# Attention and mixture of experts in one kernel: the last four attention pairs run without an expert phase between them

## The chip, the cores and the metric

The kernel runs on one NeuronCore of one Trainium2 chip. The metric is the time of one execution on the device in microseconds (us). A profile is one execution recorded by the hardware: every instruction with its engine, start and duration, and every DMA packet. The engines are named as in the profile: PE (TensorE matmul), PEld (its weight load), DVE (VectorE), ACT (ScalarE), POOL (GpSimd), SP (SyncE, which issues DMAs here). "L407" is line 407 of the kernel. Each engine executes its own instructions in the order in which they were issued to it.

## The reference, cut to what matters

Multi-query attention (16 heads, one key and value head for each of 8 batches, 384 positions, head size 64) gives 3072 tokens of 1024 features. Each token then passes a two-level gate: the best of 4 groups, and the best of 4 experts in it. The chosen expert is two 1024x1024 matrices with a ReLU between them.

```python
scores = scale * np.matmul(q, k.transpose(0, 1, 3, 2))
attn = softmax(scores)
x = np.matmul(attn, v)            # as (3072, 1024)
g_idx = np.argmax(x @ w_group, axis=1)
for g in range(G):
    xg = x[g_idx == g]
    e_idx = np.argmax(xg @ w_expert[g], axis=1)
    for e in range(Eg):
        h = np.maximum(xg[e_idx == e] @ w1[g, e], 0.0)
        out[tokens] = (g_w * e_w)[:, None] * (h @ w2[g, e])
```

All tensors are fp32. The kernel computes attention and gates in fp32 and the experts in bf16.

## The kernel before

**Pairs.** The attention is cut into 24 pairs p = 3b + st, for batch b (0 to 7) and a third st (0 to 2) of its 384 queries. A pair has six steps j. `scores(p, j)` makes scores for 64 keys (four matmuls, shown by the profile as eight) and ACT takes their exponential into a `pt` tile. `values(p, j)` multiplies it with v. `pre_add` sums the six `pt` tiles on DVE, `fold_keys`, `join` and `invert` make the reciprocal row sums, and `weigh` writes the result to `xT`; POOL casts it to the bf16 tile `xbf` (L301), and after the third of a batch SP stores that to the DRAM buffer `x_bf` (L303). The loop of pair p runs the scores of p together with the values of p - 1.

**Gates.** `gate_a` multiplies `xT` with the gate weights (64 matmuls in the profile, L312). `choose_a` takes the first third of a batch alone, `counts(now, ...)` counts its tokens by expert with a matmul (L338), and `choose_b` picks the most frequent expert, reads its number into a register of POOL and issues the load of its weights from POOL: w1 in four pieces of 512 KB (L145) and w2 in one piece of 2048 KB (L357), sizes as they arrive in SBUF, in bf16; in DRAM they are fp32 and twice as large. `gate_logits`, `gate_math` and `counts(..., full)` do the rest of a batch's gates once all three thirds exist. The weight pool has two buffers for w1 and two for w2.

**Expert units.** One batch has 14 units in a list that `fill(n)` takes from: eight h units (L407, one 128-row block of the hidden layer, eight matmuls) and six y units (L417, half of the 1024 outputs of 128 tokens, eight matmuls). They are y00, y01, y10, y11, y20, y21 by third and half below. SP stores a third after its second half (L441).

**Phases.** Six times, after pairs 4, 7, 10, 13, 16 and 19, one batch's 14 units run as a phase, and the gates of the next batch are placed inside it. After pair 22 there is a shorter phase of the eight h units of batch 6, with the gates of batch 7 inside. The order of the rest is written out by hand after the loop: the remaining units of batch 6 and the 14 of batch 7, mixed with the values of pair 23, the last gates, and the leftover pair.

**The leftover pair.** Tokens that did not choose their batch's main expert form (batch, expert) pairs. `early_pair` finds one such pair and reads its number into registers of POOL, DVE and SP. `leftover_w1` and `leftover_w2` load its expert's weights from POOL (L145, L574): the first is called once all h units of batch 6 have run (it takes that batch's w1 buffer), the second once batch 6 has finished (it takes its w2 buffer). The pair's batch is read back from `x_bf` as `xe` (L656), its tokens are turned (`pb`, L717), ranked and picked (`pr` L672, `pg` L691, `px` L726), and passed through the expert: `ph` (L735, reads w1), `phT` (L741), `py` (L749, reads w2). The result `yc` goes to the tokens in two ways: an indirect DMA of POOL to DRAM (L755) for all tokens but the last 128, and for those 128 `spread` (matmuls `lo`, L458), whose result is added when y20 and y21 of batch 7 are written (`merge`, L449). Any further pair is left to a conditional block at the end.

Of the kernel before, what the change touches and what calls it, by code (L numbers as in the profile page):

```python
# [13 lines left out]
P = 128  # L14
# [7 lines left out]
def kernel(  # L22
# [25 lines left out]
    CW = 512  # L48
# [27 lines left out]
    def side(shape, dtype, name):  # L76
        return ps_s.tile(shape, dtype, tag="s", name=name)
# [351 lines left out]
    def first_units(b):  # L429
        rows = {}  # L430

        def place(st, cs):
            if cs.start == 0:
                rows[st] = pool.tile([P, Dm], FP32, tag="y", bufs=3, name="y")
            return rows[st][:, cs]

        def store(st, cs, y):
            if closes(st):
                nc.sync.dma_start(out=outv[b, :, st, cs], in_=y)
            elif cs.stop == Dm:  # L440
                nc.sync.dma_start(out=outv[b, :, st, :], in_=rows[st][:])  # L441

        def closes(st):
            return b == B - 1 and st == ST - 1

        def merge(st, cs, ps, y):
            if not closes(st):
                return False
            nc.vector.scalar_tensor_tensor(out=y, in0=ps[:], scalar=gsel[b][:, st:st + 1], in1=leftover["y"][:, cs], op0=OP.mult, op1=OP.add)  # L449
            return True  # L450
        return moe_units(wts[b][0], wts[b][1], xbf[b], lambda: gsel[b], place, store, merge, lambda st, nh: 2 if closes(st) and nh == 1 else 1)

    def spread():
        lo = [ps_m.tile([P, 2, CW], FP32, tag="o", name="lo"), side([P, 2, CW], FP32, "lo2")]
        for i in range(2):
            for c in (i, 2 + i):
                r = slice(CAP * c, CAP * c + CAP)
                nc.tensor.matmul(out=lo[c // 2][:, c % 2, 0:QW], lhsT=leftover["spread"][r, :], rhs=leftover["yc"][r, :], start=True, stop=True, tile_position=(CAP * c, 0))  # L458
        t = pool.tile([P, Dm], FP32, tag="pt", bufs=9, name="yl")
        for i in range(2):  # L460
            nc.scalar.copy(out=t[:, i * CW:(i + 1) * CW].rearrange("p (c n) -> p c n", c=2), in_=lo[i][:, :, 0:QW])
        leftover["y"] = t
# [13 lines left out]
    def fill(n):  # L476
        while n > 0:
# [10 lines left out]
            if ran[0] == (FO + 2 * ST) * (B - 1):  # L488
                leftover_w2()

    def gates(b):
        if b == 0:
            choose_a(0, gate_a(0, 0, 1))
            return
        ps = gate_a(b, 0, ST)
        choose_a(b, ps)
        gate_logits(b - 1, ps, 1, ST)
        gate_math(b - 1)
# [25 lines left out]
    PHASES[ST + 1] -= 3  # L524
    PHASES[NP - 2] = FO

# [9 lines left out]
    def early_pair():  # L536
        last = B - 1
        mask = pool.tile([P, GE], FP32, tag="mask", bufs=1, name="mask1")
        idf = pool.tile([P, 1], FP32, tag="idf", bufs=1, name="idf1")
        nc.vector.tensor_copy(out=idf[:], in_=choice[last][:, 0:1])  # L540
        nc.vector.tensor_scalar(out=mask[:], in0=iota16[:], scalar1=idf[:, 0:1], scalar2=None, op0=OP.is_equal)
        nc.vector.scalar_tensor_tensor(out=extra[:, last * GE:NPAIR], in0=seen[last], scalar=0.0, in1=mask[:], op0=OP.is_gt, op1=OP.subtract)
        known = pool.tile([P, 1], FP32, tag="known", bufs=1, name="known")
# [32 lines left out]
    for p in range(NP):  # L576
        b, st = divmod(p, ST)
        jobs = [lambda: gates(0), lambda: None, lambda: counts(0, None)] if p == 2 else []
        if p == 0 or p == ST or (st == 1 and 1 < b < B - 1):
# [14 lines left out]
        for j in range(KB):  # L594
            if p > 0:
                values(p - 1, j)
            if j == 2 and p > 0:
                join(p - 1)
            if j + 3 < KB:
                scores(p, j + 3)  # L600
            if 0 < j < 4:
                pre_add(p, j + 2)
            if j == 2 and p > 0:
                invert(p - 1)
            if j == 3:
                stats_q(p)
                if p == 1:
                    turn_q(2, lambda h: q_raw[0][:, 2, h], [nc.scalar.copy])
                elif p == 2:
                    turn_q(3, lambda h: q_nat[0][:, h], [nc.scalar.copy])  # L610
            if jobs:
                jobs.pop(0)()
            if p == ST + 1 and j == 0:
                fill(3)
            if st == 1 and 0 < b < B - 1 and j == 0:
                load_k(b + 1)
            if 0 < j < 5:
                some_q(1 if p <= ST + 1 else 2)
            if st == 1 and b + 1 < B and j == KB - 1:
                load_v(b + 1)  # L620
        assert not jobs
        if p > 0:
            weigh(p - 1)
        fold_keys(p)
        if st == 2 and b + 1 < B:
            stats_k(b + 1)
        if p in PHASES:
            n = PHASES[p]
            steps = {}
            prep_q(p + 1)  # L630
            if b == B - 1:
                steps = {1: lambda: gates(b), 2: lambda: counts(b, None), 3: lambda: (counts(None, b - 1), early_pair())}
            else:
                steps = {2: lambda: gates(b), 4: lambda: (counts(b, b - 1), turns(p))}
            for i in range(n):
                fill(1)
                if i in steps:
                    steps[i]()
    fill(3)
    for j in range(KB):  # L640
# [4 lines left out]
    weigh(NP - 1)  # L645
    last = B - 1
    fill(2)
    gate_logits(last, gate_a(last, 1, ST), 1, ST)
    gate_math(last)
    bound_a()  # L650
    fill(2)
    counts(None, last)
    bound_b()

    xe = pool.tile([P, KO, S], BF16, tag="qraw", bufs=2, name="xe")
# [11 lines left out]
    nc.vector.tensor_add(out=mb[:, 1, 3:4], in0=mb[:, 1, 2:3], in1=m[:, 2:3])  # L667
    nfl = pool.tile([P, 1], FP32, tag="nfl", bufs=1, name="nfl")
    nc.vector.reduce_sum(out=nfl[:], in_=extra[:], axis=AX)
    fill(1)  # L670
# [4 lines left out]
    nc.vector.tensor_copy(out=rk[:], in_=pr[:, 0:4])  # L675

    small = pool.tile([P, 2], FP32, tag="small", bufs=1, name="small")
# [4 lines left out]
    for st in range(ST):  # L682
        nc.vector.tensor_scalar(out=pick[:, st, :], in0=rank_of[:], scalar1=rk[:, st:st + 1], scalar2=m[:, st:st + 1], op0=OP.is_equal, op1=OP.mult)
    pick_bf = pool.tile([P, ST, CAP], BF16, tag="kT", name="pick_bf")
    nc.vector.tensor_copy(out=pick_bf[:], in_=pick[:, :, 0:CAP])
    of_last = pool.tile([P, 2, P], FP32, tag="presum", bufs=1, name="of_last")
    nc.vector.tensor_scalar(out=of_last[:, 0, :], in0=pick[:, ST - 1, :], scalar1=leftover["final"][:, 0:1], scalar2=None, op0=OP.mult)
    fill(2)
    pg = side([P, CW], FP32, "pg")
    for st in range(ST):  # L690
        nc.tensor.matmul(out=pg[:, 0:2], lhsT=pick[:, st, :], rhs=gi[:, st, :], start=(st == 0), stop=(st == ST - 1))  # L691
    gc = pool.tile([P, 2], FP32, tag="gc", bufs=1, name="gc")
    nc.vector.tensor_copy(out=gc[:, 0:1], in_=pg[:, 0:1])
    nc.vector.tensor_scalar(out=gc[:, 1:2], in0=pg[:, 1:2], scalar1=4.0, scalar2=quarter[:, 0:1], op0=OP.mult, op1=OP.add)
    rows = pool.tile([P, 1], U32, tag="rows", bufs=1, name="rows")
    nc.vector.tensor_copy(out=rows[:], in_=gc[:, 1:2])

    nc.tensor.transpose(out=pg[:, P:2 * P], in_=of_last[:, 0, :], identity=ident[:])
    nc.vector.tensor_copy(out=of_last[:, 1, :], in_=pg[:, P:2 * P])
    leftover["spread"] = of_last[:, 1, :]  # L700

    nc.vector.tensor_sub(out=small[:, 1:2], in0=nfl[:], in1=small[:, 0:1])
    nex = pool.tile([1, 1], I32, tag="nex", bufs=1, name="nex")
# [6 lines left out]
    nc.vector.tensor_copy(out=rarei[:], in_=raref[:, 0:1])  # L710
    fill(1)

    xtok = []
    for st in range(ST):
        pb = side([P, Dm], BF16, "pb")
        for ko in range(KO):
# [3 lines left out]
        xtok.append(xt)  # L720
        fill(1)
    assert len(units) == 2 * ST
    px = side([P, KO, CAP], FP32, "px")
# [5 lines left out]

    fill(1)  # L730
    w1c, w2c = leftover["w1"], leftover["w2"]
# [11 lines left out]
    nc.vector.tensor_copy(out=hc[:], in_=phT[:])  # L743
    fill(1)
    py = side([P, QW], FP32, "py")
# [5 lines left out]
    nc.scalar.activation(out=yc[:], in_=py[:], func=ACTF.Copy, scale=gc[:, 0:1])  # L751
    leftover["yc"] = yc
    fill(1)
    spread()
    nc.gpsimd.indirect_dma_start(out=out4[0:4 * (N - P)], out_offset=bass.IndirectOffsetOnAxis(ap=rows[:], axis=0), in_=yc[:], in_offset=None, bounds_check=4 * (N - P) - 1, oob_is_err=False)  # L755
    fill(1)
    rare = nc.values_load(rarei[0:1, 0:1], min_val=0, max_val=2, skip_runtime_bounds_check_because="a sum of two comparisons")  # L757
    fill(1)

    def load_pair(pair):  # L760
# [145 lines left out]
```

## Time and profile before

| | |
|---|---|
| time, three runs | 463.19, 463.54, 464.66 us (median 463.54) |
| profiled execution | 463.94 us; span of the core 462.4 us |
| PE busy | 449.4 us, 97% |
| DVE busy | 308.8 us, 67% |
| ACT busy | 241.6 us, 52% |
| POOL busy | 60.4 us, 13% |
| DMA | 74.55 MB by the packets, mean 161 GB/s |

"Busy" is time in which at least one instruction ran; a line such as "L407 PE MATMUL hps<-xbf,w x512 | 87.3, 326" says that 512 matmuls of that line took 87.3 us in union and 326 ns in the mean each (they overlap). Times within the execution count from its first instruction. A DMA queue's share is the busy time of its packets over 16 engines; it can pass 100%, since packets overlap.

### The profile page before, as it was taken

How to read it: one execution, taken by the hardware profiler on the slowest of the kernel's cores; microseconds unless marked ns; L12 is line 12 of the kernel's file. 1: busy time of each engine (PE TensorE's matmuls, PEld its weight loads, DVE VectorE, ACT ScalarE, POOL GpSimd, SP SyncE). 2: the span in 40 equal slices, each digit the busy share in tenths (PEclk: the TensorE clock that was granted, in tenths of full speed). 3: DMA queues.
4: the chain of work that ended last, by engine and by line, in shares of the span. 5: the costliest groups of instructions: out<-in, count | busy, mean ns of one | idle time of the engine just before them, and what ended most of it. 6: DMA issues, size and time to landing. Idle time of an engine off the chain costs nothing. (4 is left out here: it accounts for less than half of the span.)

```text
span 462.4 us, 10190 instructions
## 1 busy us (share of the span) xinstructions
PE 449.4 (97%) x4196; PEld 200.4 (43%) x4208; DVE 308.8 (67%) x489; ACT 241.6 (52%) x345; POOL 60.4 (13%) x83
## 2 busy tenths in 40 slices
PE   8999999999999999999999999999999999999893
PEld 6334445333643345433543336433453335434551
DVE  4899965499708985199834997089852999554511
ACT  2966643676347743566436763477435664532231
POOL 1004003000210103000030002101030001501000
PEclk9999999999999999999999999999999999999998
DMA  8688997997599296993979566992969910999952
GB/s 164 92 141 116 217 215 106 262 191 150 95 197 251 53 205 93 246 197 89 152 121 272 109 139 106 216 243 44 199 100 252 188 69 2 162 217 268 270 134 104
DMA packets 152454, 74.55 MB, mean 161 GB/s; under 512 B 120256, under 2 KB 138944, under 8 KB 152400
## 3 DMA queue, kind: packets, MB, share of 16 engines
q0 software_dynamic: 28416, 37.81, 48.0%
q1 hardware_dynamic: 122656, 35.68, 33.0%
q8 instruction: 35, 0.57, 0.5%
q10 hardware_dynamic: 1328, 0.33, 0.4%
q14 instruction: 19, 0.16, 0.1%
HBM read 92.62 MB, written 19.01 MB: 241 GB/s over the span
## 5 line engine op out<-in xcount | busy, mean ns | idle before, releaser
L253 ACT ACTIVATE pt<-s 128x1024 f32<-128x1024 f32 x144 | 142.1, 1026 | 71.9 <-PE s L251 71.2
L251 PE MATMUL s<-qT,kT 64*64 64x512 f32 x1152 | 142.4, 594 | 0.3 <-ACT qT L229 0.2
L290 PE MATMUL o<-pt,v 64*64 64x512 f32 x1152 | 141.1, 590 | 0.0
L261 DVE TENSOR_TENSOR presum<-presum,pt 128x1024 f32<-128x1024 f32 x96 | 116.6, 1215 | 15.2 <-ACT pt L253 9.8
L407 PE MATMUL hps<-xbf,w 128*128 128x384 bf16 x512 | 87.3, 326 | 0.4 <-ACT hT L408 0.4
L417 PE MATMUL yps<-w,hT 128*128 128x512 bf16 (+1 forms) x380 | 84.6, 375 | 0.6
L259 DVE TENSOR_TENSOR presum<-pt 128x1024 f32<-128x1024 f32 x24 | 29.4, 1223 | 76.8 <-ACT pt L253 75.4
L290 PEld LDWEIGHTS o<-pt,v 64*64 64x64 f32 x1152 | 43.4, 133 | 76.8 <-issue 73.0
L251 PEld LDWEIGHTS s<-qT,kT 64*64 64x64 f32 x1152 | 40.8, 133 | 66.8 <-issue 60.0
L407 PEld LDWEIGHTS <-w 128*128 128x128 bf16 x512 | 48.1, 98 | 38.1 <-issue 7.3
L301 POOL CAST xbf<-xT 128x1024 bf16<-128x1024 f32 x24 | 25.0, 1041 | 302.7 <-DVE xT L300 302.7
L419 ACT ACTIVATE y<-yps,gsel 128x512 f32<-128x512 f32 x46 | 31.6, 687 | 56.9 <-PE yps L417 55.3
L408 ACT ACTIVATE hT<-hps 128x384 bf16<-128x384 f32 x64 | 31.2, 488 | 55.6 <-PE hps L407 52.4
L417 PEld LDWEIGHTS <-hT 128*128 128x128 bf16 x392 | 37.7, 98 | 44.6 <-issue 2.4
L145 POOL DMA_DIRECT2D w<-in_moe_w_dram x36 | 24.8, 707 | 58.1 <-DVE gsel L395 37.7
L300 DVE TENSOR_TENSOR xT<-o,rinv 128x1024 f32<-128x1024 f32 x24 | 29.2, 1215 | 2.5 <-PE o L290 2.5
L280 DVE STREAM_TRANSPOSE rinv<-rc 128x1024 f32<-128x1024 f32 x24 | 29.9, 1245 | 0.8
L265 DVE TRANSPOSE_TENSOR_REDUCE fold<-presum 128x32 f32<-128x1024 f32 x24 | 29.6, 1232 | 0.0
L243 DVE STREAM_TRANSPOSE qT<-qraw 128x1024 f32<-128x1024 f32 x20 | 23.6, 1202 | 0.0
L209 ACT ACTIVATE qraw<-qraw 128x1024 f32<-128x1024 f32 x21 | 22.0, 1049 | 0.0
L273 PEld LDWEIGHTS sm<-fold,sel 64*64 64x64 f32 x192 | 7.3, 133 | 13.3 <-issue 13.3
L312 PE MATMUL gps<-xT,gw 128*32 128x96 f32 (+2 forms) x576 | 12.6, 239 | 0.0
(152 smaller groups left out, 152.9 us busy)
## 6 DMA issues: line engine op xcount, KB each, us to landing
w<-in_moe_w_dram POOLq DMA_DIRECT2D x36, 512.0 KB, 11.3
w<-in_moe_w_dram POOLq DMA_DIRECT2D x9, 2048.0 KB, 25.9
out_dram<-y SPq DMA_DIRECT2D x23, 512.0 KB, 6.9
qraw<-in_q_dram SPq DMA_DIRECT2D x56, 192.0 KB, 3.6
x_bf<-xbf SPq DMA_DIRECT2D x8, 768.0 KB, 4.0
v<-in_v_dram SPq DMA_DIRECT2D x16, 96.0 KB, 3.1
k<-in_k_dram SPq DMA_DIRECT2D x28, 48.0 KB, 2.7
qn<-in_q_dram SPq DMA_DIRECT2D x4, 256.0 KB, 5.2
```

The lines of the kernel that those rows point to most:

```text
L251: nc.tensor.matmul(out=ps[64 * c:64 * c + 64, a, :], lhsT=kT[b][r, j * D:(j + 1) * D], rhs=qT[p][r, c * CW:(c + 1) * CW], start=True, stop ...
L253: nc.scalar.activation(out=t[:], in_=ps[:], func=ACTF.Exp, scale=scale)
L259: nc.vector.tensor_add(out=presum[p][:], in0=pt[p, 0][:], in1=pt[p, 1][:])
L261: nc.vector.tensor_add(out=presum[p][:], in0=presum[p][:], in1=pt[p, j][:])
L265: nc.vector.tensor_reduce(out=fold[p][:], in_=presum[p][:].rearrange("p a (n i) -> p (a n) i", i=32), axis=AX, op=OP.add, apply_transpose= ...
L280: nc.vector.transpose(out=t[:].rearrange("p (b i) -> p b i", i=32), in_=rc[:].rearrange("p c b -> p (c b)").unsqueeze(2).to_broadcast([P, ...
L290: nc.tensor.matmul(out=o_ps[p][64 * a:64 * a + 64, c, :], lhsT=v_sb[b][r, j, :], rhs=pt[p, j][r, a, :], start=(j == 0), stop=(j == KB - 1))
L300: nc.vector.tensor_mul(out=xT[b][:, :, ts], in0=o_ps[p][:].rearrange("p c (h n) -> p (c h) n", n=P), in1=rinv[p][:].rearrange("p (h n) -> ...
L407: nc.tensor.matmul(out=ps[:, 0:S], lhsT=w1[:, ko, fc * P:(fc + 1) * P], rhs=xb[:, ko, :], start=(ko == 0), stop=(ko == KO - 1))
L408: nc.scalar.activation(out=state["h"][:, fc, :], in_=ps[:, 0:S], func=ACTF.Relu)
L417: nc.tensor.matmul(out=ps[:], lhsT=state["h"][:, fo, st * P:(st + 1) * P], rhs=w2[:, fo, cs], start=(fo == 0), stop=(fo == FO - 1))
L419: nc.scalar.activation(out=y, in_=ps[:], func=ACTF.Copy, scale=gs_of()[:, st:st + 1])
```

## The change

The phase after pair 22 is taken out, so that pairs 20 to 23 follow each other, and the units of batches 6 and 7 (28) stand after the loop.

- The gates of batch 7 stand inside pair 23: `gate_a` at step 2 behind `scores(23, 5)`, `choose_a` at the same step, the logits of batch 6 at step 4, and `counts(7, None)`, with the weight load that it issues, behind step 5.
- `prep_q(23)`, a transpose on DVE, moves from the phase to the end of pair 20.
- `early_pair` moves from the phase to behind `counts(None, 7)`, eight units into the run, and loses the five DVE instructions that gave it batch 7's flags from the first third alone; the reduction `nfl` goes, `known` serves in its place.
- Ahead of `py` stand 26 of the 28 units, where before it was 25: y11 is moved ahead of `py`. `ph` stands behind 22 units (before: 23), `px` behind 15 (before: 22).
- The indirect DMA stands right behind `yc` instead of behind `spread`, and `spread` stands behind y20 instead of ahead of it.
- The merge with `lo` is split: y20 is scaled by ACT as other units, DVE adds `lo` to it and SP stores it (`spread`), and only y21 merges as before; ACT copies half of `lo`.

```diff
         def store(st, cs, y):
             if closes(st):
-                nc.sync.dma_start(out=outv[b, :, st, cs], in_=y)
+                if cs.start == 0:
+                    leftover["row"] = y
+                else:
+                    nc.sync.dma_start(out=outv[b, :, st, cs], in_=y)
...
         def merge(st, cs, ps, y):
-            if not closes(st):
+            if not closes(st) or cs.start == 0:
                 return False
...
-        t = pool.tile([P, Dm], FP32, tag="pt", bufs=9, name="yl")
-        for i in range(2):
-            nc.scalar.copy(out=t[:, i * CW:(i + 1) * CW].rearrange("p (c n) -> p c n", c=2), in_=lo[i][:, :, 0:QW])
+        row = leftover["row"]
+        nc.vector.tensor_add(out=row.rearrange("p (c n) -> p c n", c=2), in0=row.rearrange("p (c n) -> p c n", c=2), in1=lo[0][:, :, 0:QW])
+        nc.sync.dma_start(out=outv[B - 1, :, ST - 1, 0:CW], in_=row)
+        t = pool.tile([P, CW], FP32, tag="pt", bufs=9, name="yl")
+        nc.scalar.copy(out=t[:].rearrange("p (c n) -> p c n", c=2), in_=lo[1][:, :, 0:QW])
...
     PHASES[ST + 1] -= 3
-    PHASES[NP - 2] = FO
...
+            if p == NP - 1 and j == 2:
+                gps = gate_a(b, 0, ST)
...
+            if p == NP - 1 and j == 2:
+                choose_a(b, gps)
...
+            if p == NP - 1 and j == 4:
+                gate_logits(b - 1, gps, 1, ST)
         assert not jobs
+        if p == NP - 1:
+            counts(b, None)
...
+        if p == NP - 4:
+            prep_q(NP - 1)
...
-            if b == B - 1:
-                steps = {1: lambda: gates(b), 2: lambda: counts(b, None), 3: lambda: (counts(None, b - 1), early_pair())}
...
-    fill(3)
+    last = B - 1
+    fill(2)
+    gate_math(last - 1)
     for j in range(KB):
...
     weigh(NP - 1)
-    last = B - 1
-    fill(2)
-    gate_logits(last, gate_a(last, 1, ST), 1, ST)
-    gate_math(last)
     bound_a()
+    fill(1)
+    counts(None, last - 1)
+    fill(1)
+    rest_of_gates(last)
+    bound_b()
     fill(2)
     counts(None, last)
-    bound_b()
-
+    early_pair()
+    fill(2)
     xe = pool.tile([P, KO, S], BF16, tag="qraw", bufs=2, name="xe")
...
     for st in range(ST):
+        fill(1)
         pb = side([P, Dm], BF16, "pb")
...
-        fill(1)
-    assert len(units) == 2 * ST
+    fill(1)
     px = side([P, KO, CAP], FP32, "px")
...
-    fill(1)
+    fill(FO - 1)
     w1c, w2c = leftover["w1"], leftover["w2"]
     ph = side([P, QW], FP32, "ph")
...
-    fill(1)
+    fill(3)
     py = side([P, QW], FP32, "py")
...
     leftover["yc"] = yc
+    nc.gpsimd.indirect_dma_start(out=out4[0:4 * (N - P)], ...)
     fill(1)
     spread()
-    nc.gpsimd.indirect_dma_start(out=out4[0:4 * (N - P)], ...)
-    fill(1)
     rare = nc.values_load(rarei[0:1, 0:1], ...)
     fill(1)
```

More of the change, by code (lines that the diff above doesn't have):

```diff
@@ L435, in place, with closes @@
             return rows[st][:, cs]
+        def closes(st):
+            return b == B - 1 and st == ST - 1
         def store(st, cs, y):
             if closes(st):
-                nc.sync.dma_start(out=outv[b, :, st, cs], in_=y)
+                if cs.start == 0:
+                    leftover["row"] = y
+                else:
+                    nc.sync.dma_start(out=outv[b, :, st, cs], in_=y)
             elif cs.stop == Dm:
                 nc.sync.dma_start(out=outv[b, :, st, :], in_=rows[st][:])
-        def closes(st):
-            return b == B - 1 and st == ST - 1
         def merge(st, cs, ps, y):
-            if not closes(st):
+            if not closes(st) or cs.start == 0:
                 return False
-            nc.vector.scalar_tensor_tensor(out=y, in0=ps[:], scalar=gsel[b][:, st:st + 1], in1=leftover["y"][:, cs], op0=OP.mult, op1=OP.add)
+            nc.vector.scalar_tensor_tensor(out=y, in0=ps[:], scalar=gsel[b][:, st:st + 1], in1=leftover["y"][:, cs.start - CW:cs.stop - CW], op0=OP.mult, op1=OP.add)
             return True
@@ L489, in fill, with rest_of_gates @@
                 leftover_w2()
+    def rest_of_gates(b):
+        gate_logits(b, gate_a(b, 1, ST), 1, ST)
+        gate_math(b)
     def gates(b):
-        if b == 0:
-            choose_a(0, gate_a(0, 0, 1))
-            return
         ps = gate_a(b, 0, ST)
@@ L536, in early_pair @@
     def early_pair():
-        last = B - 1
[L538 to L542, printed above, removed]
         known = pool.tile([P, 1], FP32, tag="known", bufs=1, name="known")
@@ L577 @@
         b, st = divmod(p, ST)
-        jobs = [lambda: gates(0), lambda: None, lambda: counts(0, None)] if p == 2 else []
+        jobs = [lambda: choose_a(0, gate_a(0, 0, 1)), lambda: None, lambda: counts(0, None)] if p == 2 else []
         if p == 0 or p == ST or (st == 1 and 1 < b < B - 1):
@@ L630 @@
             prep_q(p + 1)
-            if b == B - 1:
-                steps = {1: lambda: gates(b), 2: lambda: counts(b, None), 3: lambda: (counts(None, b - 1), early_pair())}
-            else:
-                steps = {2: lambda: gates(b), 4: lambda: (counts(b, b - 1), turns(p))}
+            steps = {2: lambda: gates(b), 4: lambda: (counts(b, b - 1), turns(p))}
             for i in range(n):
@@ L645 @@
     weigh(NP - 1)
-    last = B - 1
-    fill(2)
-    gate_logits(last, gate_a(last, 1, ST), 1, ST)
-    gate_math(last)
     bound_a()
+    fill(1)
[3 more added lines that the diff above has]
+    bound_b()
     fill(2)
     counts(None, last)
-    bound_b()
+    early_pair()
+    fill(2)
     xe = pool.tile([P, KO, S], BF16, tag="qraw", bufs=2, name="xe")
@@ L667 @@
     nc.vector.tensor_add(out=mb[:, 1, 3:4], in0=mb[:, 1, 2:3], in1=m[:, 2:3])
-    nfl = pool.tile([P, 1], FP32, tag="nfl", bufs=1, name="nfl")
-    nc.vector.reduce_sum(out=nfl[:], in_=extra[:], axis=AX)
     fill(1)
@@ L683 @@
         nc.vector.tensor_scalar(out=pick[:, st, :], in0=rank_of[:], scalar1=rk[:, st:st + 1], scalar2=m[:, st:st + 1], op0=OP.is_equal, op1=OP.mult)
+    of_last = pool.tile([P, 2, P], FP32, tag="presum", bufs=1, name="of_last")
+    nc.vector.tensor_scalar(out=of_last[:, 0, :], in0=pick[:, ST - 1, :], scalar1=leftover["final"][:, 0:1], scalar2=None, op0=OP.mult)
     pick_bf = pool.tile([P, ST, CAP], BF16, tag="kT", name="pick_bf")
     nc.vector.tensor_copy(out=pick_bf[:], in_=pick[:, :, 0:CAP])
-    of_last = pool.tile([P, 2, P], FP32, tag="presum", bufs=1, name="of_last")
-    nc.vector.tensor_scalar(out=of_last[:, 0, :], in0=pick[:, ST - 1, :], scalar1=leftover["final"][:, 0:1], scalar2=None, op0=OP.mult)
     fill(2)
@@ L691 @@
         nc.tensor.matmul(out=pg[:, 0:2], lhsT=pick[:, st, :], rhs=gi[:, st, :], start=(st == 0), stop=(st == ST - 1))
+    nc.tensor.transpose(out=pg[:, P:2 * P], in_=of_last[:, 0, :], identity=ident[:])
     gc = pool.tile([P, 2], FP32, tag="gc", bufs=1, name="gc")
@@ L696 @@
     nc.vector.tensor_copy(out=rows[:], in_=gc[:, 1:2])
-    nc.tensor.transpose(out=pg[:, P:2 * P], in_=of_last[:, 0, :], identity=ident[:])
     nc.vector.tensor_copy(out=of_last[:, 1, :], in_=pg[:, P:2 * P])
     leftover["spread"] = of_last[:, 1, :]
-    nc.vector.tensor_sub(out=small[:, 1:2], in0=nfl[:], in1=small[:, 0:1])
+    nc.vector.tensor_sub(out=small[:, 1:2], in0=leftover["known"][:], in1=small[:, 0:1])
     nex = pool.tile([1, 1], I32, tag="nex", bufs=1, name="nex")
@@ L752 @@
     leftover["yc"] = yc
+    nc.gpsimd.indirect_dma_start(out=out4[0:4 * (N - P)], out_offset=bass.IndirectOffsetOnAxis(ap=rows[:], axis=0), in_=yc[:], in_offset=None, bounds_check=4 * (N - P) - 1, oob_is_err=False)
     fill(1)
     spread()
-    nc.gpsimd.indirect_dma_start(out=out4[0:4 * (N - P)], out_offset=bass.IndirectOffsetOnAxis(ap=rows[:], axis=0), in_=yc[:], in_offset=None, bounds_check=4 * (N - P) - 1, oob_is_err=False)
-    fill(1)
     rare = nc.values_load(rarei[0:1, 0:1], min_val=0, max_val=2, skip_runtime_bounds_check_because="a sum of two comparisons")
     fill(1)
+    assert ran[0] == UNITS * B
     def load_pair(pair):
```

## The prediction

> **What bounds the kernel now.** I read the page first: PE is busy for 97% of the span, so what can be won is idle PE time or time behind PE's last matmul.
>
> ```profile
> PE 449.4 (97%) x4196; PEld 200.4 (43%) x4208; DVE 308.8 (67%) x489; ACT 241.6 (52%) x345; POOL 60.4 (13%) x83
> ```
>
> The stretch that changes begins where pair 22 ends (384.15 us). I read its PE timeline from there to the end, then the waits of the same stretch.
>
> ```profile
> 373.62 2.75 PE L251 MATMUL s<-qT,kT 64*64 64x512 f32 x24
> ...
> 384.15 2.77 PE L407 MATMUL hps<-xbf,w 128*128 128x384 bf16 x16
> 386.85 1.53 PE L312 MATMUL gps<-xT,gw 128*32 128x96 f32 x64
> ...
> 447.48 1.06 PE L749 MATMUL py<-w,hc 128*32 128x256 bf16 x32
> 448.47 1.90 PE L417 MATMUL yps<-w,hT 128*128 128x512 bf16 x8
> 450.30 0.71 PE L458 MATMUL lo<-yc,of_last 32*128 32x256 f32 x8
> ```
>
> Start to start, a pair takes 384.15 - 373.62 = 10.53 us, the gate matmuls 1.46 (to the next h unit at 388.31), a y unit 450.30 - 448.47 = 1.83. py starts at 447.48, and the span ends 14.96 us later. Idle PE time in this stretch is small: 1.20 us ahead of pr (mb), 0.83 ahead of pb (xe), 0.39 and 0.37 ahead of an h unit and of pg's turn, 2.8 in all.
>
> The third view decides: POOL's timeline and the DMA queues.
>
> ```profile
> 392.78 2.73 POOL L145 DMA_DIRECT2D w<-in_moe_w_dram  x4 [5.67 <-DVE gm L393]
> 395.46 0.94 POOL L357 DMA_DIRECT2D w<-in_moe_w_dram  x1
> 396.63 2.05 POOL L145 DMA_DIRECT2D w<-in_moe_w_dram  x3 [0.24 <-PE hps L407]
> ...
> 424.88 0.88 POOL L574 DMA_DIRECT2D w<-in_moe_w_dram  x1 [4.80 <-PE yps L417]
> ```
>
> These are batch 7's w1 and w2, the leftover's w1, and its w2. The queues between 394 and 446 us:
>
> ```profile
> DMA  5999999999999999999999999999999999999940
> GB/s 76 189 163 172 193 205 203 200 207 220 208 213 214 211 213 191 265 310 210 205 206 206 245 355 336 342 313 324 234 357 332 216 213 214 217 211 210 216 91 14
> ...
> q0 software_dynamic: 6304, 8.39, 92.6%
> q1 hardware_dynamic: 720, 3.15, 15.7%
> ```
>
> The engines are full without a gap from the first packet of batch 7's w1 to the last of the leftover's w2. q0 is these four loads, 8.39 MB; q1 is SP's traffic: x_bf, xe and batch 6's three output rows. The leftover's w2 lands 20.8 us after its issue (source view of L574), at 424.88 + 20.8 = 445.7, and py, which reads it, starts at 447.48. So PE sets the end, but a full transfer queue stands only 1.8 us behind it, and what matters is when that queue starts.
>
> **What the Trainium skill says.** "DMA: Bandwidth & Descriptors", section "Bandwidth", gives a ceiling of 435 GB/s for transfers into SBUF. The trace agrees: where q0 runs alone the packets move 211 to 213 GB/s, counted in bf16; the source is fp32, so 425 GB/s are read. The stream can't run faster to make up for a late start. Its section "Queues, rings and completion order" says that each DMA engine takes turns between the queues that have work. The trace agrees: between 422 and 434 us q1 moved 2.54 MB and q0 only 1.16 MB, where alone it moves 12 x 0.2115 = 2.54. So 2.54 MB on q1 took 1.38 MB, or 6.5 us, from the loads: 2.6 us for each MB. A store from SP therefore delays the weights. Its section "Latency and other measured facts" gives about 600 ns for a register load; the trace has 0.56 us on SP and 0.69 on POOL, and shows none on DVE that delays anything.
>
> **The change part by part.** Durations come from the profiled execution (span 462.4, its run 463.94, the three runs 463.19 to 464.66); I add the difference to the median 463.54.
>
> 1. *Later weights of batch 7.* PE enters pair 23 at 384.15 instead of 396.26. One pair and the gates put the count matmul of L338 at 384.15 + 10.53 + 1.46 = 396.1. In the phase at pair 19, L338 started at 338.33, DVE's maximum at 339.16 and POOL's first load at 340.7, 2.4 us in all. So the first load is issued at 398.5 instead of 392.78: 5.7 us later. DVE is ready: behind the gate matmuls it has four small steps of choose_a and one addition left before PE passes the last values.
>
> 2. *The stream stays full.* The leftover's w1 needs h7 of batch 6 and the register. Two h units of 1.3 (398.8), values and join of pair 23 (417.56 - 412.13 = 5.4, to 404.2), h, h, gates of 1.03, h, h put L340's count for batch 7 at 410.8. DVE then has gate_c (1.1 us) and early_pair up to the index (known, the maximum and its index, 1.0), POOL its register load and issue, 1.7: about 414.8, while batch 7's own 4.2 MB keep q0 full until 420. The leftover's w2 waits for y21 of batch 6 at about 427, while its w1 needs q0 until about 439. The same 3.15 MB of q1 come meanwhile: x_bf from 407, xe from 415, the three rows to 427. So the stream has the same length and ends 5.7 us later: w1 at 434 + 5.7 = 439.6 (last packet of its quarters about 433.6), w2 at 445.7 + 5.7 = 451.4.
>
> 3. *What PE does meanwhile.* Without any wait py would start at 447.48 - 2.8 (all idle time gone) + 1.8 (y11 now ahead of it) = 446.5, up to 447.5 with a wait of 1 us at pr, where DVE's register load now stands ahead of the copy that feeds it. Ahead of this, ph is ready at about 438.2 and waits 1.4 us for w1. Then come ph 1.0, y00, phT 0.1, y01, y10, y11: PE is through at 448 and waits for w2. This wait is new.
>
> 4. *Two output rows join the stream.* y01 ends at about 444.4 and y11 at 448, so SP stores batch 7's rows 0 and 1 (0.52 MB each) in front of the last weights; before, they were issued at 446.46 and 451.1, behind them. At 2.6 us for each MB that is 1.4 each, 2.7 in all: w2 lands at 454.1. Bounds: none (both rows late or hidden), or 3.4 (the rate from 414 to 417 us, where 0.43 MB cost 1.4).
>
> 5. *Behind py.* One y unit fewer: 1.8 less. DVE's addition of lo and ACT's half copy take the place of a merge of 0.75 and a copy of the other half, beside y21's 1.76; nothing there. The indirect DMA waited before until 454.88, for the landing of row 1 by my reading; now that row is old, and it starts with yc and leaves the last stores alone. These took 3.1 us from their last issue to the end of waiting at 458.99. I take 0.4 off (0 to 0.9).
>
> 6. *Hidden or tiny.* The five DVE instructions and nfl (1.5 us) were in DVE's idle time ahead of pair 23 or behind mb. prep_q(23), 1.2 us of DVE at the end of pair 20, meets a DVE with some 0.5 us of slack in each pair: it may hold PE at the next values for 0 to 0.3 us. The switch from the phase's bf16 to the pair's fp32 matmuls goes (pair 23 took 10.59 behind it): below 0.2. POOL's cast of pair 22 queues behind the five loads, 4 us late, and nobody needs it before x_bf's store at 407.
>
> Sum against the span: +5.7 (start) + 2.7 (rows) - 1.8 (slack at py) - 1.8 (unit behind py) - 0.4 = +4.4 us.
>
> **The rivals.** *A, the forecast:* the weights arrive last, span +4.4, time 468.0 us. Its own range is +2 to +6.5 (start shift 5 to 6.5, rows 0.7 to 3.4).
>
> *B, the gaps close and nothing else decides:* PE sets py at 446.5 to 447.5, then the time is 447.0 - 447.48 - 1.8 - 0.4 = -2.7: 460.8 us. For it speaks that PE is 97% busy and that the removed idle time is real. Against it, the stream would have to be 7 us shorter, and it is at its ceiling. It decides from the point where w2 lands before 447.5, that is, with a start at most 1.8 us later than before. This is the rival on the other side.
>
> *C, late weights without the rows:* the rows' packets come behind w2 or cost the loads nothing, and the start slips by 4.5 to 5.5. Then +0.5 to +1.7, 464.0 to 465.2 us, about the size that can still be told from no change (0.3%, 1.4 us, is about what a measurement of this kernel can tell).
>
> *D, the change does not take the phase's place as said:* the order of instructions on each engine shows the gates behind the last scores of pair 23 and 28 units behind the loop, so I exclude it.
>
> **How the numbers follow.** A gets 0.75, C 0.14 (mostly within 0.3%), B 0.11. Prediction 468.0. The range reaches down through C towards B's edge, 462.5, and up to A's upper end with 0.3 for the pairs, 470.2. Faster 0.12, within 0.3% 0.13, slower 0.75.
>
> **What would show it.** In the profile after: POOL's first load of batch 7 near 398.5; the DMA row full to about 454; PE idle for some 6 us ahead of py, a wait put down to the DMA of w that the second leftover load issues, and about 1 us ahead of ph; py near 454 and the span's end 12.8 us behind it; the indirect DMA shortly behind yc. I am wrong if py starts before 449.5, if the loads start before 395, or if the transfers end early though SP's rows lie among them.

## The result, and the profile after

The changed kernel takes 467.01 us (median of 6 runs, 466.52 to 467.82), the kernel before beside it 463.23 us (6 runs): ratio 1.0078, 95% interval 1.0062 to 1.0095. It is slower by 3.8 us; 468.0 was forecast. The profiled execution has a span of 466.2 us, 3.8 more than the one of before; with a time of 467.82 us it is the slowest of the six.

The page's first line of engines shows PE busy for 97% of the span as before, with 3.6 us more of it, though the matmuls of the computation are the same (the trace of before lacks the records of 12 matmuls; the weight loads count 4208 in both):

```profile
PE 453.0 (97%) x4208; PEld 201.2 (43%) x4208; DVE 308.0 (66%) x485; ACT 242.4 (52%) x345; POOL 60.5 (13%) x83
```

PE's timeline of the kernel after, from ph to the last y units (start, busy us, line, operation, in brackets the idle time ahead of it and what ended it):

```profile
439.07 0.29 PE L739 MATMUL ph<-w,xc 128*32 128x256 bf16 x2
442.80 1.89 PE L739 MATMUL ph<-w,xc 128*32 128x256 bf16 x30 [3.44 <-DMA w<-in_moe_w_dram]
444.62 3.60 PE L417 MATMUL yps<-w,hT 128*128 128x512 bf16 x8
448.01 0.42 PE L745 MATMUL phT<-ident_bf,hg 128*128 128x128 bf16 x2
448.23 5.54 PE L417 MATMUL yps<-w,hT 128*128 128x512 bf16 x24
453.70 1.06 PE L753 MATMUL py<-w,hc 128*32 128x256 bf16 x32
454.69 1.90 PE L417 MATMUL yps<-w,hT 128*128 128x512 bf16 x8
456.52 0.71 PE L461 MATMUL lo<-yc,of_last 32*128 32x256 f32 x8
```

Two matmuls of ph run, then PE waits 3.44 us: the next one reads columns that the third and fourth quarter of the leftover's w1 bring. The rest of ph and y00 then take nearly twice their usual time (1.89 and 3.60 us instead of 1.06 and 1.90). py starts without a wait, 6.2 us later than before, and 12.55 us ahead of the end (before: 14.96).

POOL's timeline, the loads and the indirect DMA:

```profile
398.61 2.73 POOL L145 DMA_DIRECT2D w<-in_moe_w_dram  x4 [10.67 <-issue]
401.29 0.93 POOL L357 DMA_DIRECT2D w<-in_moe_w_dram  x1
...
415.60 2.75 POOL L145 DMA_DIRECT2D w<-in_moe_w_dram  x4 [8.25 <-DVE gi L668]
428.52 0.89 POOL L573 DMA_DIRECT2D w<-in_moe_w_dram  x1 [10.16 <-PE pb L722]
458.67 1.09 POOL L757 DMA_INDIRECT out_dram<-yc,rows  x1 [29.26 <-DVE y L463]
```

The first load is issued at 398.61 instead of 392.78, 5.8 us later. The last quarter of w1 is issued at 417.6 and takes 25.1 us to land (source view of L145), so it lands at 442.7, just as ph goes on; w2, issued at 428.52 (L573), takes 23.5 us and lands at 452.0.

The busy time of the engines in four stretches (us; the third column from the right is the granted PE clock):

```profile
439.00:442.80 3.80, 0.36 (x4) 0.10 (x3) 0.00 (x0) 0.49 (x1) 0.00 (x0) 0.87 1.18 211
442.80:444.60 1.80, 1.80 (x30) 1.11 (x30) 0.00 (x0) 0.00 (x0) 0.00 (x0) 0.50 1.13 214
444.60:448.20 3.60, 3.60 (x12) 1.38 (x11) 0.00 (x0) 0.39 (x1) 0.00 (x0) 0.50 1.12 213
448.20:453.70 5.50, 5.50 (x28) 2.34 (x26) 0.29 (x1) 2.06 (x3) 0.00 (x0) 0.96 0.68 180
```

The clock is halved from about 441.8 to 448.6; it falls 1.0 us ahead of the end of the wait. These slow matmuls are most of PE's extra busy time on the page. The DMA share stays above 1 through the first three stretches: the transfers are what is waited for.

The halved clock seems not to belong to every execution. Of the six runs, three show a mean granted clock of 0.988 to 0.991 and times of 467.21 to 467.82 us, three of 0.994 to 0.995 and 466.52 to 466.81 us. Half the clock for 6.8 of 466 us takes about 0.007 off the mean (an estimate from the profile), so the latter three seem to have kept it. They are 0.8 us faster by the medians, and still 3.3 us slower than the kernel before.

### The profile page after: what moved, and what is told of

Read it like the earlier page. It is cut to its first block, busy times and chain, and to the rows that moved or that the text cites. A ratio compares the mean times of both kernels' runs of the same rounds, so it can differ in the third digit from the quotient of the medians.

```text
span 466.2 us, 10202 instructions
## 1 busy us (share of the span) xinstructions
PE 453.0 (97%) x4208; PEld 201.2 (43%) x4208; DVE 308.0 (66%) x485; ACT 242.4 (52%) x345; POOL 60.5 (13%) x83
## 4 chain that ended last, share of the span: by engine, by line
PE 89%; DMA 7%; issue 1%; DVE 0%; ACT 0%; POOL 0%; ACTq 0%; POOLq 0%
PE s L251 27%; PE o L290 27%; PE hps L407 15%; PE yps L417 15%; DMA w<-in_moe_w_dram 5%; PE gps L312 3%; DMA qn<-in_q_dram 1%; PE qps L228 1%; DMA out_dram<-y 1%; PE ph L739 0%; PE sm L273 0%; ACTq L123 0%; POOL out_dram L757 0%; ACT y L419 0%; ACT hT L408 0%
## 5 line engine op out<-in xcount | busy, mean ns | idle before, releaser
L417 PE MATMUL yps<-w,hT 128*128 128x512 bf16 (+1 forms) x392 | 87.3, 380 | 0.0
L301 POOL CAST xbf<-xT 128x1024 bf16<-128x1024 f32 x24 | 25.1, 1045 | 288.2 <-DVE xT L300 288.2
L145 POOL DMA_DIRECT2D w<-in_moe_w_dram x36 | 24.8, 709 | 70.8 <-DVE gsel L395 37.6
```

Source lines behind the costliest of these rows:

```text
L417: nc.tensor.matmul(out=ps[:], lhsT=state["h"][:, fo, st * P:(st + 1) * P], rhs=w2[:, fo, cs], start=(fo == 0), stop=(fo == FO - 1))
```

## The experiments

The theory to test: the weight loads of batch 7 and of the leftover are one stream of fixed length behind the issue of L145; the change starts it 5.8 us later, and PE meets its end, which halves the clock on top. The rivals: the order of the units or the run of pairs costs the time, not the loads; or the wait at ph alone does it and could be filled.

**Fill the idle time at ph.** The edit to the kernel after, where the extra matmuls' result is read by nobody:

```diff
     fill(FO - 1)
     w1c, w2c = leftover["w1"], leftover["w2"]
+    idle = side([P, CW], FP32, "idle")
+    for _ in range(15):
+        nc.tensor.matmul(out=idle[:], lhsT=ones_bf[:], rhs=xtok[0][:, 0:CW], start=True, stop=True)
     ph = side([P, QW], FP32, "ph")
```

> The kernel after, with 15 extra bf16 matmuls of 512 columns (about 3.3 us) between the last h unit and ph; nobody reads what they write. They fill the 3.4 us in which PE waits for the leftover's w1 and cannot move its landing. Theory (late weights, and a clock that halves behind PE's idle stretch): ph still runs its third matmul at about 442.8, but the clock stays full, ph takes 1.0 us instead of 1.9 and y00 1.8 instead of 3.4, py starts at about 451.5 or when w2 has landed (452.0), and the time falls by 1.5 to 2.8 us against the kernel after, to about 464.5 to 465.5. Rival (ph and y00 were slow because of the transfers that run beside them, not of the idle stretch): they stay slow, and the time stays at 467 us.

Measured 466.12 us, ratio to the kernel before 1.0053 (1.0035 to 1.0071). Its PE timeline:

```profile
440.16 3.40 PE L738 MATMUL idle<-xt,ones_bf 128*128 128x512 bf16 x14
443.49 1.06 PE L742 MATMUL ph<-w,xc 128*32 128x256 bf16 x32
444.48 1.90 PE L417 MATMUL yps<-w,hT 128*128 128x512 bf16 x7
...
452.88 1.06 PE L756 MATMUL py<-w,hc 128*32 128x256 bf16 x32 [1.20 <-DMA w<-in_moe_w_dram]
```

ph and y00 are back at 1.06 and 1.90 us, with the clock full in this profile, while the transfers run beside them as before, so the transfers did not slow them; the idle stretch did. The time fell by 0.9 us by the medians and by 1.2 by the ratios, less than the 1.5 expected, and its interval overlaps that of the kernel after a little. PE reaches py at 451.7, 2.0 us sooner, but waits 1.2 us there for w2. The next stage of the same stream takes back more than half of the gain. Against the three runs of the kernel after that seem to have kept the clock, the gain is 0.4 us.

**Only the loads late, in the kernel before.**

```diff
-steps = {1: lambda: gates(b), 2: lambda: counts(b, None), 3: lambda: (counts(None, b - 1), early_pair())}
+steps = {1: lambda: gates(b), 6: lambda: (counts(b, None), counts(None, b - 1), early_pair())}
```

The count of batch 6 and `early_pair`, which followed it at the third step, move along.

> The kernel before with one edit: the count that issues batch 7's weight loads, and early_pair behind it, stand four h units later in the phase (behind the seventh unit). Nothing else moves. Theory (the start of the weight stream decides): the first load is issued at about 398 instead of 392.8, the stream ends about 5.2 us later, w2 lands at about 451, PE waits some 3.4 us ahead of py, and the time rises by 3 to 5 us, to 466.5 to 468.5 us. Rival (the run of four pairs and the new order of units cost the time, not the loads): within 0.7 us of the kernel before, 463 to 464 us.

Measured 466.25 us, ratio 1.0074 (1.0048 to 1.0101), just below the range; PE waits 2.5 us at py, not 3.4. The first load is issued at 397.19, 4.4 us late (not 5.2: in its old place the count had waited for DVE). With the phase, the pairs and the units where they were, this edit alone costs as much as the whole change. Its wait:

```profile
450.31 1.06 PE L749 MATMUL py<-w,hc 128*32 128x256 bf16 x32 [2.48 <-DMA w<-in_moe_w_dram]
```

It stands at py, as w1 came in time there, and the clock stays full behind 2.48 us of idle time (1.06 for py).

**Only the loads early, in the kernel after.**

```diff
+        if p == NP - 1:
+            gps = gate_a(b, 0, ST)
+        pre_add(p, 1)
+        if p == NP - 1:
+            choose_a(b, gps)
+            gate_logits(b - 1, gps, 1, ST)
+        pre_add(p, 2)
...
             if j + 3 < KB:
                 scores(p, j + 3)
+            if p == NP - 1 and j == 0:
+                counts(b, None)
```

(The same calls behind scores 5 and values 4 and 5 go.)

> The kernel after with the gates of batch 7 placed earlier in pair 23: gate_a ahead of the first values, choose_a and the logits of batch 6 behind the first addition, the count that issues the loads behind scores 3. The four pairs stay in a row and the units stay one run. Theory (late loads alone made the change slow): the first load is issued at 392.8 to 394, w1 of the leftover lands before ph is ready at about 439, PE never waits more than 1 us, py starts at about 447, and the time is 2 to 3.5 us below the kernel before: 460 to 461.5 us. Rival (order of the units, or contention of rows with the stream): 464 us or more although the loads start early.

Measured 461.40 us, ratio 0.9967 (0.9950 to 0.9983): 1.5 us below the kernel before by the ratio, 5.6 below the kernel after by the medians. POOL and PE in its timelines:

```profile
392.85 2.73 POOL L145 DMA_DIRECT2D w<-in_moe_w_dram  x4 [5.37 <-issue]
```

```profile
438.95 1.06 PE L738 MATMUL ph<-w,xc 128*32 128x256 bf16 x32
...
447.06 1.06 PE L752 MATMUL py<-w,hc 128*32 128x256 bf16 x32
```

No wait at ph or py: the run of four pairs and of 28 units, with the end of the change, is the better order, and rival B of the prediction (py at 446.5 to 447.5, 460.8 us) describes this kernel. The change paid for it with the place of its gates. How much of the 1.5 us is the end's is told below.

**Two places between.** In the early-gates kernel, the count behind scores 4 or scores 5:

```diff
-            if p == NP - 1 and j == 0:
+            if p == NP - 1 and j == 1:
                 counts(b, None)
```

(`j == 2` in the second.)

> The kernel of the early gates with one edit: the count that issues batch 7's loads stands behind scores 4 of pair 23 instead of scores 3, about 1.9 us later (first load at 394.7 instead of 392.85). In the early-gates kernel py started as w2 landed, with nothing to spare, and ph had some 1.4 us to spare. Theory (the start of the loads sets the end, one us for one us): py waits about 1.5 to 2 us for w2, and the time is 1.2 to 2 us above the early gates' 461.4: 462.6 to 463.4 us, about the kernel before. Rival (several us of slack remain, only a wait of 3.4 us that halves the clock costs much): 461.4 to 462.0 us.

> The same with the count behind scores 5, about 3.7 us later (first load at 396.5). Theory (one us for one us): w1 of the leftover lands about 441 and ph waits 2 us, py starts about 450.5, the clock stays full, and the time is 3 to 4 us above the early gates' 461.4: 464.4 to 465.4 us. Rival (slack, and a cost only with the halved clock): below 463.5 us.

Measured 462.73 us (ratio 0.9984, 0.9972 to 0.9997) and 463.77 us (0.9998, 0.9990 to 1.0007), with first loads at 395.03 and 397.01. The first is in its range, but by luck: no wait for weights shows in its profile, where w2 landed at 447.8 and PE came to py at 448.85. The second lies between its own range and the rival's: 4.2 us of lateness cost 2.4 us by the medians, 1.4 by the ratios. ph had no wait there, py 1.1 us:

```profile
450.07 1.06 PE L752 MATMUL py<-w,hc 128*32 128x256 bf16 x32 [1.11 <-DMA w<-in_moe_w_dram]
```

Part of the cost is thus not the stream's: PE reached ph 1.8 us later than with early gates in both profiles, by waits for xT (0.4 and 1.1 us, as the maximum for the loads stands ahead of weigh on DVE), for xe, and a later pair 23. So "one us for one us" is not shown; what is shown is that the last step is the steepest. From 397.0 to the kernel after's 398.6 it is 1.6 us more of lateness for 3.2 us more of time, as the wait at ph and the halved clock set in.

**The end of the change alone, and the early gates without it.** The first is the kernel before with y11 ahead of py, the indirect DMA right behind yc, spread behind y20 and the split merge; the second is the early-gates kernel with these four undone.

```diff
-    fill(1)
+    fill(2)
     py = side([P, QW], FP32, "py")
...
     leftover["yc"] = yc
+    nc.gpsimd.indirect_dma_start(out=out4[0:4 * (N - P)], ...)
     fill(1)
     spread()
-    nc.gpsimd.indirect_dma_start(out=out4[0:4 * (N - P)], ...)
-    fill(1)
```

> The kernel before with the end of the change alone: y11 ahead of py, the indirect DMA right behind yc, spread behind y20, y20 scaled by ACT with lo added by DVE. The phase behind pair 22 and its loads stay. Theory: py starts 1.8 us later (449.3), what follows it is 2.2 to 2.5 us shorter, so the time is 0.3 to 0.8 us below the kernel before: 462.4 to 462.9 us. Rival (the tail edits cost time, the addition and its store at the very end): 0.3 us or more above the kernel before.

> The early-gates kernel with the end of the kernel before: y11 behind py, the indirect DMA behind spread, y20 and y21 both merged by DVE. py is then ready 1.7 us earlier, at 445.3, but its w2 lands at about 447, so PE waits 1.7 us, and y11 and the store of row 1, on which the indirect DMA waits, come about 2.7 us later. Theory (y11 ahead of py fills the wait for w2, and row 1's store ends the chain): 1.5 to 2.7 us above the early gates: 462.9 to 464.1 us. Rival (the end's edits are worth the 0.5 us that they brought alone): 461.6 to 462.2 us.

Measured 463.12 us (ratio 0.9990, 0.9980 to 1.0000) and 462.82 us (0.9983, 0.9976 to 0.9990). Alone the end is worth about 0.5 us, hardly to be told from nothing; in the early-gates kernel its loss costs 1.4 us by the medians, 0.7 by the ratios, between the theory's range and the rival's. So of the 1.5 us that the early gates win by the ratio, the run of pairs and units alone is worth 0.8. py waited only 0.34 us for w2 there, not 1.7: PE reached it at 446.1, 0.8 later than assumed.

**Still earlier, and xe's wait filled.** choose_a ahead of the first addition, the count ahead of scores 3, two y units ahead of the first turn of xe.

> The early-gates kernel with two edits: choose_a ahead of the first addition and the count right behind values 0, ahead of scores 3 (loads about 0.7 us earlier, for a PE stall of 0.3 us or less), and two y units instead of one ahead of the first turn of xe, which waited 0.9 us for its DMA. Theory (the stream and PE end together there, both have to come forward): 0.4 to 0.9 us below the early gates, 460.5 to 461.0 us. Rival (the end is set by the store of row 1 and the indirect DMA behind it, or by PE's total): no change, 461.2 to 461.6 us.

Measured 461.94 us, ratio 0.9960 (0.9946 to 0.9974): no change against the early gates that can be told, and a median above both ranges. In its profile the loads did not come earlier (393.95: PE had entered pair 23 0.7 us later in this execution), and row 1's store, now issued at 447.6 with the loads ending at 447.3, took 4.9 us to land instead of 3.5. The indirect DMA follows that landing. PE, 0.2 us sooner at ph, also waited 0.7 us ahead of py; the profile puts this down to ACT, but w2 landed at 447.56 and py started at 447.61. So the PE time won was handed back at both places.

**Real work at ph instead of idle time, and the same with py's wait filled.** In the kernel after, y00 and y01 ahead of ph; the second kernel has 19 extra matmuls, read by nobody, ahead of py.

```diff
-    fill(FO - 1)
+    fill(FO + 1)
     w1c, w2c = leftover["w1"], leftover["w2"]
...
-    fill(3)
+    fill(1)
     py = side([P, QW], FP32, "py")
```

and in the second kernel also

```diff
+    idle = side([P, CW], FP32, "idle")
+    for _ in range(19):
+        nc.tensor.matmul(out=idle[:], lhsT=ones_bf[:], rhs=xtok[0][:, 0:CW], start=True, stop=True)
     py = side([P, QW], FP32, "py")
```

> The kernel after with y00 and y01 moved from behind ph to ahead of it, so that PE has real work while the leftover's w1 lands; the loads stay late. PE is then through with all units at about 448 and waits there for w2 (landed at 452.0 in the kernel after). Theory (the load stream is the bound, the order of the units can't help): py not before 452, and the 4 us of idle PE halve its clock now at py and y20, so 466 to 468.5 us, no better than the kernel after by more than 1 us. It also tests the prediction's price for the rows: row 0 is stored at about 443, well inside the stream; if a row costs the loads 1.4 us each, the last packet of w2 ends 53 us or more behind the stream's first one, if it costs nothing, 51 to 52 us as in the kernels so far. Rival (the wait at ph alone made the change slow): 462 to 464 us.

> The same with 19 extra bf16 matmuls of 512 columns (4.1 us) ahead of py, which nobody reads, so that PE does not idle while w2 lands. Theory: the clock stays full, py starts when w2 has landed, 452 to 453.5, and the time is that of the kernel after with PE kept busy at ph, 465.3 to 466.8 us; if the kernel without these matmuls had the halved clock, it is 1.5 to 3 us slower than this one. Rival (the halved clock plays no part): both within 0.5 us of each other.

Measured 470.82 us (ratio 1.0149, 1.0132 to 1.0166) and 470.14 us (1.0139, 1.0122 to 1.0156), both above what I expected, and worse than the change itself. In the first kernel:

```profile
455.35 1.90 PE L753 MATMUL py<-w,hc 128*32 128x256 bf16 x32 [7.51 <-DMA w<-in_moe_w_dram]
```

and its stretches show what kept w2:

```profile
448.00:452.00 4.00, 0.00 (x0) 0.00 (x0) 0.00 (x0) 0.57 (x1) 0.00 (x0) 1.00 1.09 269
452.00:456.00 4.00, 0.65 (x16) 0.58 (x20) 0.00 (x0) 0.00 (x0) 0.00 (x0) 0.61 0.30 107
```

PE has nothing to run from 448 to 452, and the DMA engines are full at 269 GB/s, above the 213 of the loads alone: two output rows run among them (the first until 450.2, the second from 451.3). Packet times in the trace give the length of the load stream, from the first packet of batch 7's w1 to the last of the leftover's w2:

| kernel | first load issued | packets of the loads | length | median, us |
|---|---|---|---|---|
| before | 392.78 | 394.2 to 445.4 | 51.2 | 463.2 |
| early gates | 392.85 | 394.3 to 446.5 | 52.2 | 461.4 |
| count behind scores 4 | 395.03 | 396.4 to 447.5 | 51.1 | 462.7 |
| count behind scores 5 | 397.01 | 398.4 to 449.8 | 51.4 | 463.8 |
| before, loads late | 397.19 | 398.8 to 449.9 | 51.1 | 466.3 |
| after | 398.61 | 400.0 to 451.7 | 51.7 | 467.0 |
| after, kept busy at ph | 399.03 | 400.5 to 452.5 | 52.0 | 466.1 |
| after, y00 and y01 ahead of ph | 398.55 | 400.0 to 454.9 | 54.9 | 470.8 |

Seven orders of the work give the same stream, 51.1 to 52.2 us, and so do the three kernels that the table leaves out (end alone, old end, still earlier: 51.2 to 51.8); its end moves with its start. Only where rows 0 and 1 are both stored inside it does it grow, by 3.2 us against the kernel after; in the second kernel of this pair it is 54.6. The rival that the wait at ph alone made the change slow falls: filled with real work it costs more, as PE waits longer at py and the rows come early. Without the 3.2 us of the rows py would have started at about 452.1 (an estimate), still 4.7 us later than in the kernel before.

The comparison of these two kernels says little on the clock. The extra matmuls ended 3.37 us ahead of py; of the second kernel's four runs one took 468.77 us at a mean clock of 0.996, three took 470.1 to 470.2 at 0.992 to 0.993, so most seem to have lost the clock for a while. The profile is of the fastest one: there it stayed full, with 3.37 us of idle time. The three others are 1.4 us slower. The rival there (both within 0.5 us) is neither confirmed nor excluded by the medians, which are 0.7 us apart.

## Why the prediction was right, and where its steps were not

The direction, the cause (the late load stream) and the size held: +4.4 us forecast on the span, +3.8 measured. The path by which the late loads reached the end was another one in part. Forecast was a wait of some 6 us at py, for w2 behind two output rows; the profile has a wait of 3.4 us at ph, for w1, then half the clock, and none at py. Step by step:

1. *Later weights.* Forecast 398.5, measured 398.61. That it matters is shown from both sides: late loads alone make the kernel before slow, early loads alone make the kernel after fast.
2. *The stream stays full and keeps its length.* Right within 0.6 us; w2 landed at 452.0 against 451.4 without rows. (`early_pair` stands behind six units of the run, not eight as said ahead; the leftover's w1 is loaded behind eight.)
3. *What PE does meanwhile.* The wait at ph was forecast at 1.4 us and was 3.44. The mis-sized term is w1's landing, 439.6 in the forecast and 442.7 in the profile: I had read its landing in the kernel before from the bytes moved, as 434, but loads overlap in the queue. There the last quarter's packets ran to 435.4, and it landed at 398.97 + 36.7 = 435.7. That is 1.7 of the 3.1 us; the rest is not traced. The halved clock was not in the sum, though the sum had PE idle for 6 us: ph, y00 and phT took 5.4 us from 442.80 to 448.23 where the kept-busy kernel needs 2.8, so 2.6 us in the profiled execution. About 0.8 us of it stays in the time, by the runs with and without it.
4. *The rows.* Wrong for this kernel, right in price. I had rows 0 and 1 stored at 445 to 449, inside the stream, and py waiting for w2 to 454.1. With PE held at ph they were stored at 451.1 and 454.5 behind w2's packets (last at 451.7), and py did not wait at all. In place of the +2.7 us of this step stand 2.3: w2 landed 0.6 us later than forecast without rows, and PE, held up by the wait at ph and the slow clock, came to py 1.7 us behind that landing. That the two are near each other is luck, and it made the total better than its parts. The kernel with y00 and y01 ahead of ph shows the mechanism: +3.2 us for two rows against the 2.7 forecast.
5. *Behind py.* Forecast -2.2, measured 12.55 - 14.96 = -2.4. But the indirect DMA did not start with yc. It was issued 1.1 us after row 1 landed (454.5 + 3.0 against 458.67), and with such a delay of 1.1 to 1.2 us in every profile but the last two, where row 1 had landed earlier and it followed yc. What shortened the end is one y unit fewer, 1.8 of the 2.4 us; the rest is not traced.
6. *Hidden parts.* Right in the main: PE entered pair 23 at 384.52 instead of 384.15, which is no more than executions with the same code up to there differ (384.07 to 384.95). The wait at pr was 0.15 us, where up to 1 was allowed for. Of POOL's ten register loads in the kernel before, eight took 0.29 to 0.30 us; the 0.69 that the prediction names is the longest. Nothing in the sum rests on it.

No stream ran faster to make up for a late start, and the 425 GB/s of fp32 that the loads read (twice the 211 to 213 GB/s in bf16) stay below the Trainium skill's 435 GB/s ("DMA: Bandwidth & Descriptors", section "Bandwidth"). That figure is for the ports into SBUF, where the same loads arrive as 211 to 213 GB/s, so that it was the limit is not shown; the length of the stream is. For the halved clock, "TensorE: Matmul & The Clock Gate", section "What's actually happening", says that the array runs at half its clock by default, that a free-running window of about 3.4 us without enough work brings it back to that, and a busy one releases it. The profile agrees: half clock for some 6.8 us, two such windows, behind 3.44 us of idle time, and none behind 2.48. How much idle time in a window is needed can be read from the traces, in the last section.

## What to carry to other kernels

When a step issues loads that a full transfer queue serves, its place fixes the end of the whole queue: compare that end with the first reader before moving it, and move the rest of the phase without it if need be. Read a load's landing from its own issue-to-landing time, not from the bytes that the queue has moved, as the last packets straggle into the next load. Before filling a wait with other work, ask which stores that work releases and whether the reader behind it waits for the same queue.

## What the runs showed of the hardware

**The clock.** A wait of 3.44 us cost PE another 2.6 us through the clock, and one of 7.51 us showed 1.90 us for py instead of 1.06; one of 2.48 us cost nothing further, and one of 3.37 neither. The length of the wait alone does not decide. In all twelve profiles the granted clock, once full, changes only at whole steps of 3.413 us: in the kernel after it is full from 4.88 us on, falls 128 steps later at 441.79, and is back 2 steps later at 448.62. Two steps of the kernel after, up to and behind the fall, and two of the second kernel with real work at ph, around its wait of 3.37 us (columns as above):

```profile
438.38:441.79 3.41, 0.98 (x7) 0.34 (x5) 0.00 (x0) 0.49 (x1) 0.00 (x0) 1.00 1.20 210
441.79:448.62 6.83, 5.82 (x41) 2.67 (x42) 0.15 (x1) 0.70 (x2) 0.00 (x0) 0.50 1.12 213
```

```profile
449.70:453.11 3.41, 1.99 (x10) 0.69 (x7) 0.00 (x0) 0.00 (x0) 0.00 (x0) 1.00 1.01 259
453.11:456.52 3.41, 1.41 (x34) 1.00 (x36) 0.00 (x0) 0.35 (x1) 0.00 (x0) 1.00 0.09 28
```

In the kernel after, PE was idle for 3.41 - 0.98 = 2.43 us of one step, and the clock fell at its end. In the other kernel the grid cut the wait in two, with 1.42 and 2.00 us of idle time in the two steps, and the clock stayed. Over the twelve profiles, every full-clock step with 2.07 us or more of idle PE was followed by half the clock (the least is in the kernel with the count behind scores 4, at 452.89 to 456.31, where PE ended its work), and none with 2.00 us or less. That a wait of some 3.4 us lost the clock in some runs of a kernel and not in others fits this, as the wait falls on the grid in another place; for these runs it is not shown.

**Stores beside loads.** Two output rows of 0.52 MB, stored while the loads ran, lengthened these by 3.2 us, or 1.6 each if shared evenly. A single row at the stream's end shows no price that can be told: five streams with 0.43 MB of row 0 inside took 51.1 to 52.2 us, three without any row 51.2 to 51.7. With no loads beside it such a row landed in 2.6 to 3.0 us in the kernel after and for row 1 of the kernel before, but in 5.0 for the latter's row 0.
